# Buffers of keys, queries and values of branch A released by chunk, with the planner's constants set anew

## The chip, the cores and the metric

The kernel runs on one core of one Trainium2 chip. The metric is the device time of one execution in microseconds (us); less is better. A core has TensorE (PE in the profile; its weight loads are PEld), VectorE (DVE), ScalarE (ACT), GpSimd (POOL) and SyncE (SP, which here only issues DMAs). Each engine works through its own instructions in the order in which the program lists them and waits on semaphores for the others.

## The reference

Two attention branches are computed from two inputs of 2048 x 1024 in bf16, and their outputs are put side by side. Both have 32 heads of 32 channels.

```python
# branch A: plain attention, no mask
q, k, v = split(x @ wqkv)                    # 2048 x 1024 each
p = softmax(q @ k.T * 32 ** -0.5)            # 32 heads, 2048 x 2048
a = (p @ v) @ wo
# branch B: four segments of 512 rows, causal inside one, a memory M, z carried between them
p = softmax(qs @ ks.T * scale + mask)
a_mem = (phi(qs) @ M) / (phi(qs) @ z + 1e-6)
o = g * a_mem + (1 - g) * (p @ vs)
M, z = M + phi(ks).T @ vs, z + phi(ks).sum() # phi(t) = t + 1 if t > 0 else exp(t)
b = o @ wo
out = concat([a, b], -1)
```

## The kernel before

**What is computed where.** A head group is four heads, 128 channels; branch A has groups 0 to 7. A *unit* of branch A, written A(g, c), is 256 queries (chunk c of 8) of group g against all 2048 keys. It has eight *sets*; a set is 256 keys: four PE instructions write the scores of four heads to PSUM (line 960), two exps on ScalarE, of 128 x 1024 each, turn them into P (line 1039; line 1026 for the very first ones), and eight matmuls multiply P with the values (line 1135) and with ones (line 1142), which gives the row sums. In two or three sets of most units one of the four heads goes without ScalarE: a cubic on VectorE and GpSimd (lines 997, 1000 to 1002) stands for the exp, and ScalarE's instruction is half as long. A unit of branch B, B(s, j), is two head groups of one segment in five sets. Group 0's first four chunks are done in parts, since the input is still being loaded.

**Projections.** All other PE work is cut into *jobs* of eight steps with a 512-column moving operand: keys or queries of branch A (`job_KA(g, kq, c)`, four chunks c of 512 rows for keys, kq = 0, and four for queries, kq = 1), values (`job_VA`, `job_V0`), the same for branch B (`job_KB`, `job_VB`), and the two output projections (`job_outA`, `job_outB`). Jobs share one PSUM bank, so one job is open at a time; its result leaves by a DVE cast (line 1310), after which the bank is free.

**Buffers.** Keys and queries of group g lie in slot g % 2 of `KQ_A`, values of two groups in one of two `V_A`. So the projections of group g write where the keys and queries of group g - 2 stood. Each buffer has a record per chunk of 512 rows (`r_KQA[slot][kq][c]`), by which real dependencies are kept; but the planner offers all eight jobs of group g only from 2 us after the last unit of group g - 2, `r = en["A", g - 2, 7] + 2.0`, and a score set asserts with `holds` that all eight chunks carry the tag of its group.

**The guard.** Exps run without a shift as long as a bound on the scores says that this is safe. For each group the squares of keys and queries are made on GpSimd (line 1324, a ring of four tiles `sqA`), four of them are summed on PE and reduced on VectorE (`guard_cols`, lines 1335 and 1342), and when keys and queries are both there, `guard_end` (lines 1379 to 1413) spreads the maxima through PE and writes a flag. The first exp of the group waits until VectorE has written the flag (`run_split`): ScalarE loads it and branches. A late projection is therefore a late first exp of the group.

**The order of the work.** It is made when the program is built. `plan` sorts the units by a list of numbers: groups 0 to 5 in turn, then groups 6 and 7 interleaved as `PAIR` says, with the units of branch B put in at `B_FIRST`, `B_STEP`, `B_STEP3`, `B_GAP`. Each unit gets planned start and end times `st`, `en`. `plan_jobs` offers every job with a release time, a due time (`LEAD_A` = 14.219 us ahead of the group's first unit for keys and queries) and a cost of 1.75 us; `NUDGE` shifts due times by hand. `level` spreads the jobs so that the load is as even as the windows allow, and `Prog.schedule` then builds each engine's list with a model of durations and latencies; what PE takes next is ranked by `JOB_AT`, `JOB_SLOPE`, `DUE_AT`, `AHEAD`, `HEAT` and others. The weights of a group come by two DMAs on SP (`load_WA`), 10 us ahead of the release.

Near the end the units stand so: A(5,6), A(5,7), A(6,0), A(6,1), B(3,0), A(6,2), A(7,0), B(3,2), A(7,1), A(7,2), B(3,4), A(6,3), A(7,3), B(3,6), A(6,4), A(7,4), and so on to A(6,7), A(7,7). Between the end of group 5, which frees slot 1, and the first unit of group 7, which needs it, stand four units.

Of the kernel before, what the change touches and what calls it, by code (L numbers as in the profile page):

```python
# [33 lines left out]
CUBIC = [[], [1, 3], [2, 4], [1, 3], [1, 3], [1, 3], [1, 3], [1, 3], [1, 3], [1, 3], [1, 3], [1, 3], [1, 3], [1, 3], [1, 3], [1, 3, 5]]  # L34
CHAIN = 0
CUBE_PV = 3.203
# [3 lines left out]
SOON = 0.39  # L40

PAIR = ((6, 0), (6, 1), (6, 2), (7, 0), (7, 1), (7, 2), (6, 3), (7, 3), (6, 4), (7, 4), (6, 5), (7, 5), (6, 6), (7, 6), (6, 7),
        (7, 7))
# [6 lines left out]
B_STEP3 = 1.03  # L50
# [101 lines left out]
AHEAD = 18.672  # L152
HEAT = 0.757
# [5 lines left out]
NORM_K = 8.39  # L159
JOB_AT = 0.555  # L160
JOB_SLOPE = 0.737
MARGIN = 3.147
RXJ = 4
RX0 = 34.384
LEAD_A, LEAD_B, DUE_AT, DUE_SLOPE = 14.219, 8.77, 4.982, 0.1
# [4 lines left out]
STEP = 1.785  # L170
OUT3 = 87.197
OT_STEP = 2.92
NUDGE = {('KB', 3, 1): 8.43, ('VB', 1, 1): -8.13, ('OB', 0, 0): 8.85, ('OB', 2, 0): 12, ('KB', 1, 0): 7.83, ('OA', 4): -18.13, ('KB', 3, 0): -14.16, ('KA', 5): -2.7, ('KB', 3, 2): 0.67, ('OA', 3): -1.8, ('OA', 5): 0.15, ('VB', 0, 0): -25, ('phi', 3, 1): 6.17, ('KB', 3, 3): -2.7, ('KB', 2, 2): -3.03, ('OA', 0): 0.43, ('VB', 2, 0): 3.71, ('phi', 0, 1): -1.72, ('KB', 1, 1): -2.67, ('phi', 1, 1): 6.71, ('phi', 3, 3): 4.88, ('VB', 1, 0): -3.01, ('OB', 0, 1): 5.6, ('VB', 2, 1): 1.82, ('OB', 3, 0): 0.39, ('VB', 3, 1): -7.84, ('OB', 1, 1): 0.61, ('OB', 1, 0): 4.5, ('KB', 1, 2): -4.13, ('phi', 0, 0): 6.16, ('VB', 0, 1): 9.83, ('OB', 3, 1): -2.58, ('phi', 2, 2): -0.46, ('KB', 2, 1): 4.39, ('VA', 1): 6.19, ('KA', 2): -1.14, ('KA', 6): -6.01}
SAFE = 0
WOA_STEP = 3
OUT_D = 57.959
M_AT = 4.042

# [387 lines left out]
class _Kernel:  # L566
# [214 lines left out]
    def plan(self):  # L781
        self.plan_constants()
        T = 0.0
        self.st, self.en = {}, {}
        self.sets = {}
        self.slot_n = 0
# [129 lines left out]
    def plan_set(self, take, T):  # L916
# [16 lines left out]
        def f(key):  # L933
# [3 lines left out]
            for p in range(len(take[0]["pieces"])):  # L937
                for b, t in enumerate(take):
# [35 lines left out]
        u = take[0]["unit"]  # L974
        self.st.setdefault(u, T0)
# [541 lines left out]
    def job_KA(self, g, kq, c, key, behind=None):  # L1517
# [275 lines left out]
    def plan_jobs(self):  # L1793
# [13 lines left out]
        for c in (2, 3):  # L1807
            add(p2 - 3.9, p2 + 9.0, VJ, lambda key, c=c: self.job_V0(0, c, key, None, self.early_gc))
# [6 lines left out]
        for g in range(1, 8):  # L1815
            r = en["A", g - 2, 7] + 2.0 if g > 1 else 1.0
            d = st["A", g, 0] - LEAD_A
            for kq in range(2):
                self.item(r - 10.0 + kq * STEP, lambda key, g=g, kq=kq: self.load_WA(g, kq, key))
            for kq in range(2):  # L1820
                for c in range(4):
                    add(r, d, KQ, lambda key, g=g, kq=kq, c=c: self.job_KA(g, kq, c, key), "KA", g)
            add(r, d, 0.4, lambda key, g=g: self.guard_A(g, key + 2.0))
        for p in range(1, 4):
# [5 lines left out]
            for tp in range(8):  # L1830
                add(r, d, VJ, lambda key, p=p, tp=tp: self.job_VA(p, tp, key), "VA", p)
# [127 lines left out]
```

## Time and profile before

| | |
|---|---|
| median of 3 runs | 1118.94 us (1118.09 to 1119.88) |
| the profiled execution | 1119.28 us |
| its span, first to last instruction | 1117.6 us |
| ScalarE busy | 1068.5 us, 96% |
| TensorE busy | 1039.4 us, 93% |
| VectorE busy | 744.2 us, 67% |
| GpSimd busy | 675.6 us, 60% |
| mean granted TensorE clock | 0.996 |

The span is the time from the first to the last instruction of the profiled execution; 1.7 us of that execution lie around it. In a row of the timeline the columns are start, duration, engine, line, operation, output<-input, shapes, count, and in brackets the idle time of the engine before it with what ended it. A row of the waits has the waiting instruction, what it waited for, the total, the number of times and the longest. A row of the windows has the stretch, its length, and the busy time of each engine with its number of instructions, then the granted clock, the DMA share and the bandwidth. Rows of a line that is a helper (598 for the steps of all jobs, 1310 for all casts, 1324 for all squares) are told apart by the tiles.

### The profile page before, as it was taken

How to read it: one execution, taken by the hardware profiler on the slowest of the kernel's cores; microseconds unless marked ns; L12 is line 12 of the kernel's file. 1: busy time of each engine (PE TensorE's matmuls, PEld its weight loads, DVE VectorE, ACT ScalarE, POOL GpSimd, SP SyncE). 2: the span in 40 equal slices, each digit the busy share in tenths (PEclk: the TensorE clock that was granted, in tenths of full speed). 3: DMA queues.
4: the chain of work that ended last, by engine and by line, in shares of the span. 5: the costliest groups of instructions: out<-in, count | busy, mean ns of one | idle time of the engine just before them, and what ended most of it. 6: DMA issues, size and time to landing. Idle time of an engine off the chain costs nothing.

```text
span 1117.6 us, 55335 instructions
## 1 busy us (share of the span) xinstructions
PE 1039.4 (93%) x25336; PEld 555.5 (50%) x25336; DVE 744.2 (67%) x1567; ACT 1068.5 (96%) x1224; POOL 675.6 (60%) x654
## 2 busy tenths in 40 slices
PE   8999999999989989999999998989999889899997
PEld 4455545465545544455445444555555444444553
DVE  3346577765665686877875878697755777875443
ACT  4989999999999999999999999999999799999996
POOL 2224576856667576766666786676665857665530
PEclk9999999999999999999999999999999998999999
DMA  9032450024213231023241321033031450021101
GB/s 208 10 78 46 82 131 15 15 45 104 73 34 83 64 90 26 16 73 62 65 91 58 92 48 27 18 85 88 22 104 55 113 153 21 31 69 51 59 22 50
DMA packets 171099, 72.01 MB, mean 64 GB/s; under 512 B 134768, under 2 KB 169072, under 8 KB 170864
## 3 DMA queue, kind: packets, MB, share of 16 engines
q1 hardware_dynamic: 168496, 67.66, 24.6%
q8 instruction: 199, 3.26, 1.3%
q10 hardware_dynamic: 2368, 0.79, 0.3%
q14 instruction: 36, 0.29, 0.1%
HBM read 45.23 MB, written 11.67 MB: 51 GB/s over the span
## 4 chain that ended last, share of the span: by engine, by line
ACT 43%; PE 42%; DVE 11%; issue 2%; POOL 2%; ACTq 0%; DVEq 0%; POOLq 0%
ACT P L1039 41%; PE ps L598 22%; PE ps L960 8%; PE ps L1135 6%; PE ps L1142 5%; DVE Pc L1002 1%; DVE T L1160 1%; DVE PKQ_B L1605 1%; DVE rc L1167 1%; DVE Y L997 1%; ACT PKQ_B L1600 1%; PE ps L1556 1%; ACT P L1026 1%; DVE T L1163 1%; DVE outsb L1310 1%
## 5 line engine op out<-in xcount | busy, mean ns | idle before, releaser
L1039 ACT ACTIVATE P<-ps 128x1024 bf16<-128x1024 f32 (+1 forms) x1176 | 1041.2, 1078 | 27.4 <-PE ps L1142 11.3
L1142 PE MATMUL ps<-P,onesb 128*32 128x256 bf16 (+1 forms) x4628 | 298.0, 271 | 0.2 <-issue 0.2
L1000 POOL TENSOR_SCALAR Z<-Y 128x512 f32<-128x512 f32 x118 | 182.1, 1544 | 155.7 <-DVE Y L997 140.8
L1135 PE MATMUL ps<-P,V_A 128*32 128x256 bf16 x3860 | 255.0, 275 | 5.9 <-ACT P L1039 2.0
L960 PE MATMUL ps<-KQ_A 32*128 32x256 bf16 x4096 | 204.0, 273 | 24.2 <-ACT P L1039 17.6
L1001 POOL TENSOR_TENSOR Z<-Z,Y 128x512 f32<-128x512 f32 x118 | 152.0, 1288 | 4.1
L1142 PEld LDWEIGHTS ps<-P,onesb 128*32 128x32 bf16 x4628 | 129.6, 97 | 35.9 <-issue 13.5
L960 PEld LDWEIGHTS ps<-KQ_A 32*128 32x128 bf16 x4096 | 61.4, 92 | 167.9 <-ACT P L1039 129.5
L598 PE MATMUL ps<-xT_B,W_B 128*32 128x512 bf16 (+1 forms) x2240 | 138.1, 365 | 4.6 <-DVE cols L1396 1.3
L598 PE MATMUL ps<-xT_A,W_A 128*32 128x512 bf16 (+1 forms) x2224 | 136.9, 364 | 4.8 <-DVE KQ_A L1310 1.2
L1135 PEld LDWEIGHTS ps<-P,V_A 128*32 128x32 bf16 x3860 | 108.6, 96 | 45.6 <-issue 14.2
L1002 DVE SCALAR_TENSOR_TENSOR Pc<-Z,Y 128x512 bf16<-128x512 f32 x118 | 110.7, 938 | 26.3 <-POOL Z L1001 19.5
L997 DVE TENSOR_SCALAR Y<-ps 128x512 f32<-128x512 f32 x118 | 80.8, 685 | 67.3 <-PE ps L960 66.4
L1059 POOL TENSOR_SCALAR_AFFINE_SELECT P<-P 128x768 bf16<-128x768 bf16 (+1 forms) x96 | 78.0, 817 | 76.5 <-ACT P L1039 75.8
L1324 POOL TENSOR_TENSOR sqA<-KQ_A 128x512 bf16<-128x512 bf16 x61 | 66.0, 1084 | 91.3 <-DVE KQ_A L1310 68.4
L1324 POOL TENSOR_TENSOR sqB<-KQ_B 128x512 bf16<-128x512 bf16 x64 | 70.0, 1097 | 51.5 <-DVE KQ_B L1310 41.0
L1160 DVE STREAM_TRANSPOSE T<-ps 128x256 f32<-128x256 f32 (+1 forms) x148 | 71.5, 485 | 17.4 <-PE ps L1142 12.4
L598 PEld LDWEIGHTS ps<-xT_B,W_B 128*32 128x32 bf16 x2240 | 51.9, 96 | 55.1 <-issue 22.3
L598 PEld LDWEIGHTS ps<-xT_A,W_A 128*32 128x32 bf16 x2224 | 51.6, 96 | 54.5 <-issue 16.9
L1310 DVE CAST KQ_B<-ps 128x512 bf16<-128x512 f32 x64 | 44.0, 687 | 46.4 <-PE ps L598 45.0
L1175 DVE STREAM_TRANSPOSE T<-rc 128x256 f32<-128x256 f32 (+1 forms) x152 | 71.7, 477 | 2.4
L598 PE MATMUL ps<-Wv_B,xT_B 128*32 128x512 bf16 (+1 forms) x1120 | 68.5, 363 | 3.9 <-DVE V_B L1310 1.7
(106 smaller groups left out, 1316.9 us busy)
## 6 DMA issues: line engine op xcount, KB each, us to landing
Wv_B<-in_B_wv_dram SPq DMA_DIRECT2D x32, 256.0 KB, 3.0
W_B<-in_B_wk_dram SPq DMA_DIRECT2D x32, 256.0 KB, 3.2
W_B<-in_B_wq_dram SPq DMA_DIRECT2D x32, 256.0 KB, 4.1
Wo_B<-in_B_wo_dram SPq DMA_DIRECT2D x32, 256.0 KB, 3.0
out_dram<-outsb SPq DMA_DIRECT2D x56, 128.0 KB, 1.8
W_A<-in_A_wqkv_dram SPq DMA_DIRECT2D x14, 256.0 KB, 4.2
ot_a_scratch<-OTst SPq DMA_DIRECT2D x50, 64.0 KB, 2.3
xT_A<-ot_a_scratch SPq DMA_DIRECT2D x6, 512.0 KB, 4.4
```

Of the source, the lines that this page charges most:

```text
L598: ins = e.matmul(out[r], w[:, r], x, start=start, stop=stop, tile_position=(0, 32 * t), skip_group_check=True)
L960: ins = e.matmul(out, kap, qap, start=st, stop=True, tile_position=(32 * h, 0), skip_group_check=True)
L997: o = self.dve(lambda e: e.tensor_scalar(Y[:, :], src, KAPPA * SCALE, -KAPPA * ROOT, ALU.mult, ALU.add), 512, key - 9.0, [self.bank[bank]] ...
L1000: self.pool(lambda e: e.tensor_scalar(Z[:, :], Y[:, :], CUBE_A, None, ALU.add), 512, key - BCK, [rY], [rZ], rate=0.38)
L1001: self.pool(lambda e: e.tensor_tensor(Z[:, :], Z[:, :], Y[:, :], ALU.mult), 512, key - BCK, [rY, rZ], [rZ], rate=0.435)
L1002: last.append(self.dve(lambda e: e.scalar_tensor_tensor(out=dst, in0=Z[:, :], scalar=CUBE_B, in1=Y[:, :], op0=ALU.add, op1=ALU.mult), 512, ...
L1039: a = self.act(guarded if early else lambda e: e.activation(dst, src, ACT.Exp, scale=SCALE), cols, key, rd, wr, fixed=EXP_FIXED)
L1059: self.pool(lambda e: e.affine_select(v, v, pattern=pat, compare_op=ALU.is_ge, fill=0.0, base=0, channel_multiplier=-1), 2 * nd * P, key + ...
L1135: ins = e.matmul(self.ps[32 * h:32 * h + 32, 512 * obk + q0:512 * obk + q0 + nq], v, p, start=first, stop=last, tile_position=(0, 32 * h), ...
L1142: ins = e.matmul(self.ps[32 * h:32 * h + 32, lcol + q0:lcol + q0 + nq], self.onesb[:, 0:32], p, start=False, stop=last, tile_position=(0, ...
L1160: self.dve(lambda e: e.transpose(T2[:, 0:n], src), n, nk, rsrc, [r2], fixed=0.17)
L1324: self.pool(lambda e: e.tensor_tensor(sq[:, :], src, src, ALU.mult), 512, key, [rsrc], [rs], rate=0.5)
```

## The change

Keys, queries and values are offered to the next owner of their buffer by chunk. For g > 1 the release of a key chunk c (kq = 0) is the planned end of set 2c + 1 of the last unit of group g - 2, of a query chunk c (kq = 1) the planned end of unit A(g - 2, 2c + 1), each plus `FREED` = 0.5 us. The query chunks may so come up to one group sooner, the key chunks within the last unit of the old group. Value chunks are treated like key chunks with `VFREED`, and never later than before. The score sets assert only the chunks that they read. The four squares of a quad are put on record together when its fourth job is, so that the ring of four tiles is never shared by two quads at once; each square still needs only its own cast. The weights are loaded 10 us ahead of the first chunk of their own half. Apart from this, some fifteen constants of the planner and the table `NUDGE` have other values, among them `PAIR`, in which A(7,3) stands ahead of A(6,3), A(7,4) ahead of A(6,4) and A(7,5) ahead of A(6,5); by `B_STEP3`, B(3,6) stands one unit later. `CUBIC` is written in another way; its first two entries differ, but the first stands for the units in parts, which it does not reach, so that the number of half-length exps is the same (118 of 1184 exps).

```diff
-B_STEP3 = 1.03
+B_STEP3 = 1.073
...
-AHEAD = 18.672
-HEAT = 0.757
+AHEAD = 23.295
+HEAT = 0.681
...
-JOB_SLOPE = 0.737
+JOB_SLOPE = 0.617
...
-LEAD_A, LEAD_B, DUE_AT, DUE_SLOPE = 14.219, 8.77, 4.982, 0.1
+LEAD_A, LEAD_B, DUE_AT, DUE_SLOPE = 14.219, 8.77, 8.001, 0.1
...
-OUT3 = 87.197
+OUT3 = 72.703
...
+V0_R = 4.52
+V0_D = 11.868
+FREED = 0.5
+VFREED = 11.963
...
@@ plan_set
-                        holds([r for x in self.r_KQA[sl] for r in x], "KQ", g)
+                        holds([self.r_KQA[sl][0][kt // 4], self.r_KQA[sl][1][q // 512]], "KQ", g)
...
+        self.tset[take[0]["set"]] = T
@@ job_KA
-        q.append(self.square("A", dst, self.r_KQA[sl][kq][c], key + 1.5))
-        if len(q) == 4 and g > 0:
-            self.colA[(g, kq)] = self.guard_cols(key + 4.0, q)
+        q.append((dst, self.r_KQA[sl][kq][c], key + 1.5))
+        if g == 0:
+            q[-1] = self.square("A", *q[-1])
+        elif len(q) == 4:
+            self.colA[(g, kq)] = self.guard_cols(key + 4.0, [self.square("A", *x) for x in q])
@@ plan_jobs
         for c in (2, 3):
-            add(p2 - 3.9, p2 + 9.0, VJ, lambda key, c=c: self.job_V0(0, c, key, None, self.early_gc))
+            add(p2 - V0_R, p2 + V0_D, VJ, lambda key, c=c: self.job_V0(0, c, key, None, self.early_gc))
...
-            r = en["A", g - 2, 7] + 2.0 if g > 1 else 1.0
+            r = [[1.0] * 4] * 2
+            if g > 1:
+                r = [[self.tset["A", g - 2, 7, 2 * c + 1] + FREED for c in range(4)], [en["A", g - 2, 2 * c + 1] + FREED for c in range(4)]]
             d = st["A", g, 0] - LEAD_A
             for kq in range(2):
-                self.item(r - 10.0 + kq * STEP, lambda key, g=g, kq=kq: self.load_WA(g, kq, key))
-            for kq in range(2):
+                self.item((max(r[kq][0] - 10.0, q2) if g > 1 else r[kq][0] - 10.0 + STEP * kq), lambda key, g=g, kq=kq: self.load_WA(g, kq, key))
                 for c in range(4):
-                    add(r, d, KQ, lambda key, g=g, kq=kq, c=c: self.job_KA(g, kq, c, key), "KA", g)
+                    add(r[kq][c], d, KQ, lambda key, g=g, kq=kq, c=c: self.job_KA(g, kq, c, key), "KA", g)
+            r = max(r[0][3], r[1][3])
             add(r, d, 0.4, lambda key, g=g: self.guard_A(g, key + 2.0))
...
             for tp in range(8):
-                add(r, d, VJ, lambda key, p=p, tp=tp: self.job_VA(p, tp, key), "VA", p)
+                rt = self.tset["A", 2 * p - 3, 7, tp] + VFREED if p > 1 else r
+                add(min(r, rt), d, VJ, lambda key, p=p, tp=tp: self.job_VA(p, tp, key), "VA", p)
```

The other constants of the planner that change (`CUBE_PV`, `SOON`, `NORM_K`, `RX0`, `OT_STEP`, `OUT_D` and the `NUDGE` table) are left out here.

More of the change, by code (lines that the diff above doesn't have):

```diff
@@ L33 @@
 KAPPA, ROOT, CUBE_A, CUBE_B = 0.5501767600212002, -1.5993248390626598, -0.9857377158509045, 1.2295944671136563
-CUBIC = [[], [1, 3], [2, 4], [1, 3], [1, 3], [1, 3], [1, 3], [1, 3], [1, 3], [1, 3], [1, 3], [1, 3], [1, 3], [1, 3], [1, 3], [1, 3, 5]]
+CUBIC = ((1, 3), (1, 3), (2, 4), (1, 3), (1, 3), (1, 3), (1, 3), (1, 3), (1, 3), (1, 3), (1, 3), (1, 3), (1, 3), (1, 3), (1, 3), (1, 3, 5))
 CHAIN = 0
-CUBE_PV = 3.203
+CUBE_PV = 3.205
 CARRY = 7
@@ L39 @@
 BCK = 9.626
-SOON = 0.39
-PAIR = ((6, 0), (6, 1), (6, 2), (7, 0), (7, 1), (7, 2), (6, 3), (7, 3), (6, 4), (7, 4), (6, 5), (7, 5), (6, 6), (7, 6), (6, 7),
-        (7, 7))
+SOON = 0.124
+PAIR = ((6, 0), (6, 1), (6, 2), (7, 0), (7, 1), (7, 2), (7, 3), (6, 3), (7, 4), (6, 4), (7, 5), (6, 5), (6, 6), (7, 6), (6, 7), (7, 7))
 BIAS_PART = (17, 16, 18)
@@ L158 @@
 PV_HOT = 1.702
-NORM_K = 8.39
+NORM_K = 8.667
 JOB_AT = 0.555
-JOB_SLOPE = 0.737
+JOB_SLOPE = 0.617
 MARGIN = 3.147
 RXJ = 4
-RX0 = 34.384
-LEAD_A, LEAD_B, DUE_AT, DUE_SLOPE = 14.219, 8.77, 4.982, 0.1
+RX0 = 34.374
+LEAD_A, LEAD_B, DUE_AT, DUE_SLOPE = 14.219, 8.77, 8.001, 0.1
 HOLD = {}
@@ L785, in plan @@
         self.sets = {}
+        self.tset = {}
         self.slot_n = 0
```

6 lines of the change are left out of this document (3 added, 3 removed).

## The prediction

> **What bounds the kernel now.** I read the page first, then ScalarE's waits.
>
> ```profile
> PE 1039.4 (93%) x25336; PEld 555.5 (50%) x25336; DVE 744.2 (67%) x1567; ACT 1068.5 (96%) x1224; POOL 675.6 (60%) x654
> ACT  4989999999999999999999999999999799999996
> ```
>
> ScalarE is busy for 1068.5 of 1117.6 us, and its 40 slices show the idle time at the start, at the end, and in one slice of the middle, the seven. Nothing else can be gained as long as the exps stay what they are, and by the forms they are fixed in number and length:
>
> ```profile
> L1039 ACT ACTIVATE P<-ps 128x1024 bf16<-128x1024 f32 x1058 | 1006.2, 1123 | 26.1 <-PE ps L1142 11.3 <-PE ps L598 8.9 <-PE ps L960 3.2
> L1039 ACT ACTIVATE P<-ps 128x512 bf16<-128x512 f32 x118 | 80.3, 680 | 1.3 <-PE ps L960 1.3
> ```
>
> The change keeps 1058 full and 118 half exps and the 8 of line 1026. So the question is what becomes of ScalarE's waits:
>
> ```profile
> ACT P L1039 <- PE ps L1142: 11.3, 15, 2.9
> ACT P L1039 <- PE ps L598: 8.9, 1, 8.9
> ACT P L1039 <- PE ps L960: 4.5, 10, 1.1
> ```
>
> One single wait is 8.9 us; the other two rows, 15.8 us together, are 25 waits of at most 2.9 us. The timeline of ScalarE places the long one, and the timeline of all engines around it shows what came before. The 58 exps before it, counted back in the plan's order, are A(6,2), B(3,0), A(6,1) and A(6,0), so that the exp at 895.86 is the first of A(7,0), and group 5 ended at about 834.8.
>
> ```profile
> 884.85 0.68 DVE L1310 CAST KQ_A<-ps 128x512 bf16<-128x512 f32 x1
> ...
> 886.23 1.49 POOL L1324 TENSOR_TENSOR sqA<-KQ_A 128x512 bf16<-128x512 bf16 x1
> ...
> 887.14 1.90 PE L598 MATMUL ps<-xT_B,W_B 128*32 128x512 bf16 x32
> ...
> 889.09 0.69 DVE L1310 CAST KQ_B<-ps 128x512 bf16<-128x512 f32 x1 [2.07 <-PE ps L598]
> ...
> 889.84 0.40 PE L1335 MATMUL ps<-sqA,blk 128*32 128x512 bf16 x4 [0.47 <-DVE KQ_B L1310]
> ...
> 893.15 0.69 DVE L1310 CAST KQ_B<-ps 128x512 bf16<-128x512 f32 x1 [1.52 <-PE ps L598]
> ...
> 893.89 0.22 PE L1388 MATMUL ps<-pick,dg 128*32 128x16 bf16 x8 [0.79 <-DVE KQ_B L1310]
> ...
> 895.22 0.15 DVE L1413 SCALAR_TENSOR_TENSOR flags<-braw,flags 128x1 int32<-128x1 f32 x1
> ...
> 895.86 1.94 ACT L1039 ACTIVATE P<-ps 128x1024 bf16<-128x1024 f32 x2 [8.90 <-PE ps L598]
> ```
>
> This is the guard of group 7. Its eighth cast lands at 885.53 (884.85 + 0.68). Then follow the square, the sum on PE, which has to let a job of branch B through the only job bank first, another such job, the spread, and the flag at 895.37: 9.8 us from the cast to the flag. ScalarE was ready at 886.96 (895.86 - 8.90). The profile puts the wait down to a PE job, but it is the flag, 0.5 us ahead of the exp, that ended it.
>
> Why the cast is late is seen in the windows (stretch, PE, PEld, DVE, ACT, POOL):
>
> ```profile
> 728.00:756.00 28.00, 24.66 (x696) 14.84 (x688) 25.65 (x53) 27.49 (x32) 21.71 (x23) 1.00 0.35 90
> 756.00:784.00 28.00, 25.48 (x669) 14.43 (x668) 22.57 (x52) 27.74 (x33) 17.97 (x19) 1.00 0.34 83
> 784.00:812.00 28.00, 26.87 (x672) 14.10 (x668) 20.32 (x42) 27.88 (x34) 19.43 (x17) 1.00 0.12 28
> 812.00:834.80 22.80, 22.80 (x551) 12.16 (x547) 11.80 (x18) 22.76 (x27) 14.14 (x13) 1.00 0.44 118
> 834.80:868.00 33.20, 32.60 (x780) 17.16 (x776) 18.24 (x36) 33.13 (x38) 19.29 (x18) 1.00 0.18 55
> 868.00:887.00 19.00, 16.45 (x424) 8.68 (x424) 17.83 (x40) 18.95 (x23) 18.00 (x20) 1.00 0.51 129
> 887.00:895.90 8.90, 6.28 (x124) 3.14 (x124) 4.53 (x15) 0.04 (x1) 4.15 (x5) 1.00 0.15 51
> ```
>
> From 812 to 868 PE has 0.6 us of idle time in 56; ScalarE does not suffer there, but jobs queue. From 728 to 812 PE idles for 7.0 us (3.34 + 2.52 + 1.13), and none of group 7's work can go there, since all of it is held until group 5 is through. Inside the full stretch the eight casts stand so:
>
> ```profile
> 851.10 0.68 DVE L1310 CAST KQ_A<-ps 128x512 bf16<-128x512 f32 x1
> ...
> 861.07 0.69 DVE L1310 CAST KQ_A<-ps 128x512 bf16<-128x512 f32 x1 [1.12 <-PE ps L598]
> 867.49 0.69 DVE L1310 CAST KQ_A<-ps 128x512 bf16<-128x512 f32 x1 [0.89 <-PE ps L598]
> ```
>
> The first four begin at 851.10 and end with 861.07; the other four run from 867.49 to 884.85.
>
> **The change part by part.** *The query half of group 7 comes sooner.* A job is 32 matmuls; the one that starts at 887.14 takes 1.90 us, and since its end is modelled and overlaps what follows, I take 1.75 us of PE, an estimate. Four query jobs are 7.0 us of PE, four casts of 0.69, four squares. They may now start behind A(5,1), A(5,3), A(5,5) and A(5,7), which by the same count end at 729, 769, 807 and 835. The idle 7.0 us of 728 to 812 are what hides them, and group 6's own query jobs leave that stretch in turn for one earlier still. What is left after 834.8 is the key half: four jobs instead of eight. From the first cast to the eighth it is 33.8 us in seven steps, 4.8 us a step; four jobs less are worth 19 us at that pace, and 13.3 us at the pace of the first four (861.07 - 851.10 = 9.97 in three steps, 3.3 us each); I take the smaller. Either is more than 8.9. With the chain of 9.8 us behind the last cast, the flag would come at 895.37 - 13.3 = 882.1, ahead of ScalarE's 886.96 by 4.9 us. **The wait goes in full: -8.9 us.**
>
> *Is PE able to follow?* After 834.8 it has 7.0 us less to do, and the 2.6 us that it idled in the wait (8.90 - 6.28) need not be spent. That is 9.6 us, more than the 8.9 by which ScalarE is now ahead. So ScalarE can keep its lead to the end without a smaller idle share of PE.
>
> *What is late next.* The flag of B(3,2)'s guard.
>
> ```profile
> 898.79 0.15 DVE L1413 SCALAR_TENSOR_TENSOR flags<-braw,flags 128x1 int32<-128x1 f32 x1
> ```
>
> Its keys stand in the same queue, and the flag is 3.6 us behind that of group 7, at 898.9, while B(3,2), 16 exps behind the one at 895.86 and by the count at 909.5, would start at 900.6. That is 1.7 us to spare even if nothing ahead of it moves, and the four jobs that left move it forward too. I cost it at nothing; without that cover it is 3.3 us, one job step.
>
> *Weights, casts and squares.* The number is the same, the places move.
>
> ```profile
> L1324 POOL TENSOR_TENSOR sqA<-KQ_A 128x512 bf16<-128x512 bf16 x61 | 66.0, 1084 | 91.3 <-DVE KQ_A L1310 68.4
> W_A<-in_A_wqkv_dram SPq DMA_DIRECT2D x14, 256.0 KB, 4.2
> ```
>
> Twelve of the 14 weight loads on SP get another time, six of them a group earlier; one lands in 4.2 us and is asked for 10 us ahead, and the DMA share of 0.08 to 0.51 in the rows above leaves room, so nothing. On SP it passes output and scratch stores, which nobody waits for there. A square is 1.08 us on GpSimd, which had 91.3 us of idle time just before squares. A quad's ring tiles are handed out at its fourth job, so a fourth square can stand behind the previous quad's sum; with quads many microseconds apart I take 0, and at most the 1.49 us of one square in the chain above, which the 4.9 us cover.
>
> *Groups 2 to 6.* None of their guards shows a long wait, so sooner projections bring nothing there but fewer full stretches. The 15.8 us of small waits are made anew by another order. The early one and the one at the clock drop are singled out below; 11.4 us are left, and I take them as unchanged, with a quarter, 2.9 us, to both sides.
>
> *The start.* The retimed values job 2 of group 0 is on the path:
>
> ```profile
> 55.75 1.96 PE L1556 MATMUL ps<-Wv_A,xT_A 128*128 128x128 bf16 x32
> ...
> 58.49 0.29 PE L1135 MATMUL ps<-P,V_A 128*32 128x256 bf16 x4 [0.78 <-DVE V_A L1566]
> ```
> ```profile
> 59.16 3.77 ACT L1039 ACTIVATE P<-ps 128x1024 bf16<-128x1024 f32 x4 [2.88 <-PE ps L1142]
> 63.33 45.15 ACT L1039 ACTIVATE P<-ps 128x1024 bf16<-128x1024 f32 x51 [0.40 <-PE ps L1142]
> ```
>
> P waits for those values, and ScalarE for P's buffers: 3.3 us. The job is released 0.6 us sooner but is due 2.9 us later (11.868 against 9.0), while the rank of jobs changes too. Bounds: -3.3 (gone) and +2.9 (the later due time in full). I take 0, since the two edits pull apart.
>
> *The clock.* One stretch runs at half the clock:
>
> ```profile
> 924.00:928.00 4.00, 2.92 (x50) 1.04 (x46) 3.93 (x12) 4.00 (x6) 4.00 (x5) 0.62 0.60 131
> 928.00:932.00 4.00, 4.00 (x68) 2.05 (x68) 3.97 (x5) 3.18 (x4) 3.49 (x4) 0.53 0.00 0
> ```
> ```profile
> 932.26 29.08 ACT L1039 ACTIVATE P<-ps 128x1024 bf16<-128x1024 f32 x33 [0.95 <-PE ps L1142]
> ```
>
> It cost ScalarE 0.95 us there. In the new order it may fall away or come elsewhere: -1.0 to +1.0, taken as 0.
>
> *Sum.* 1119.28 - 8.9 = 1110.4 for an execution like the profiled one; that one lies 0.34 above the median of 1118.94, so **1110.0 us**, 0.8% less. With all small terms good it is 1110.0 - 3.3 - 1.0 - 2.9 = 1102.8, with all bad 1110.0 + 2.9 + 1.0 + 2.9 = 1116.8.
>
> **The rivals.** *Half of it comes* (0.14). The due time of group 7 is the same, 14.2 us ahead of its first exp, and the jobs that leave may be replaced: output and value jobs of branch B close up behind, and the planner spreads what is left up to the due time. If two of the four places are filled, the flag comes 6.7 us sooner instead of 13.3, the 8.9 become 2.2, and a later guard takes about the same again: 1110.0 + 4.4 = 1114.4. For it: the stretch from 812 to 868 is full. Against: nothing in the change brings branch B's jobs forward.
>
> *The clock drops in the full stretch* (0.05). By the half clock of 924 to 932, a stretch of 6.8 us at half speed puts PE 3.4 us behind; between 812 and 868, with 0.6 us of idle, all of it would reach ScalarE: 1113.4. [...] Against: the granted clock was 1.00 there, and 0.996 over the span. [...]
>
> *It doesn't do what it says* (0.06). The query jobs are offered sooner but the order built from ranks still takes them last, or the key half alone is late: 1119 us, within 0.2%.
>
> *Slower* (0.20). The release of a query chunk is 0.5 us behind the planned end of a unit, where before it was 2 us behind a whole group. Where PE runs behind the plan, the cast stands in VectorE's list before the scores that it waits for are done. Behind it in that list stands the cubic's first step (line 997), which frees a score bank, and behind that PE's next scores:
>
> ```profile
> 420.93 4.79 ACT L1039 ACTIVATE P<-ps 128x512 bf16<-128x512 f32 x6 [1.14 <-PE ps L960]
> ```
>
> This is ScalarE's price for one late score set at a half exp, 1.14 us. There are 24 query casts in groups 2 to 7 (six times four). If more than 8 hit (8 x 1.14 = 9.1), the gain is eaten; with half of them, 13.7 us, it is 1110.0 + 13.7 = 1123.7. For it: PE is 93% busy, with full stretches. Against: a release is no start; `level` puts most jobs well behind it, and VectorE is busy only 67%.
>
> **How the numbers follow.** The forecast has 0.55. Its own range is 1103 to 1117; the half, the clock and the rival without effect lie below 1121, and what is left out is the slower one: range 1103 to 1121. This kernel's measurement can tell about 0.2%, 2.2 us: faster, below 1116.7, is 0.55 + 0.14 + 0.05 = 0.74; same is 0.06; slower, above 1121.2, is 0.20.
>
> **What would show it.** Right: no wait of ScalarE over 3 us behind the start; the first exp of A(7,0) directly behind A(6,2), at about 887; its last KQ_A cast before 877 and its flag before 887; some KQ_A casts between 729 and 835 that belong to group 7; PE's idle time from 728 to 812 smaller, and that from 834.8 to 887 larger; 1058 and 118 exps. Wrong: a wait of several us at another group's first exp; ScalarE's many small waits clearly above 15.8 us, with VectorE casts of KQ_A that waited for line 960; a wait at 55 to 64 above 3.3 us.

## The result and the profile after

The changed kernel takes 1115.89 us (median of 16 runs, 1114.80 to 1118.98), the kernel before 1119.76 us (16 runs, 1117.77 to 1125.07). The ratio is 0.9963, with a 95% interval of 0.9954 to 0.9972: 3.9 us or 0.37% less. It is faster by more than the 0.2% that can be told, and the time lies inside the range of 1103 to 1121, but the gain is 0.37% where 0.8% was forecast.

The profiled execution took 1116.0 us, 3.3 us less than that of before. The page of the changed kernel (helpers have moved down a few lines: 598 is now 601, 960 is 964, 1039 is 1044, 1142 is 1147, 1310 is 1315, 1324 is 1329, 1335 is 1340, 1413 is 1418):

```profile
span 1114.3 us, 55312 instructions
PE 1035.5 (93%) x25332; PEld 558.1 (50%) x25332; DVE 732.8 (66%) x1567; ACT 1068.6 (96%) x1224; POOL 676.3 (61%) x654
ACT  4989999999999999999999999999999899999997
```

ScalarE does the same 1068.6 us of work. The slice that held the seven is an eight: the hole is smaller, not closed. ScalarE's waits on PE in its exps say why:

```profile
ACT P L1044 <- PE ps L1147: 19.5, 22, 3.7
ACT P L1044 <- PE ps L964: 4.8, 8, 1.7
```

The row of 8.9 us, one wait on a projection job, is gone. But the row for the ones matmul went from 11.3 to 19.5 us. A fourth row of the kernel before, at the start, has no counterpart now:

```profile
ACT P L1039 <- PE ps L1556: 1.4, 1, 1.4
```

Added up, these waits were 11.3 + 8.9 + 4.5 + 1.4 = 26.1 us and are 24.3 us. By this view little was gained. ScalarE's timeline shows where a part of it went:

```profile
883.38 2.15 ACT L1044 ACTIVATE P<-ps 128x1024 bf16<-128x1024 f32 x2
887.89 1.02 ACT L1044 ACTIVATE P<-ps 128x1024 bf16<-128x1024 f32 x1 [2.37 <-PE ps L1147]
890.61 7.01 ACT L1044 ACTIVATE P<-ps 128x1024 bf16<-128x1024 f32 x8 [1.70 <-PE ps L964]
```

The first exp of A(7,0) stands inside the last row, at 894.25, and waits for nothing. Just ahead of it, in A(6,2), ScalarE waits 2.37 + 1.70 = 4.07 us, where before it waited 0.02.

The exps are the same in number and, between the marks used here, in amount, so the starts of units can be compared across kernels. Counted off in the timeline (us; the last exp is its end):

| stretch | before | after | difference |
|---|---|---|---|
| start to A(0,4) | 79.63 | 80.34 | +0.71 |
| A(0,4) to A(6,0) | 755.17 | 758.41 | +3.24 |
| A(6,0) to A(7,0) | 61.06 | 55.50 | -5.56 |
| A(7,0) to the last exp | 211.91 | 212.21 | +0.30 |
| last exp to the end | 9.79 | 7.81 | -1.98 |
| sum | 1117.56 | 1114.27 | -3.29 |

The stretch that the change aims at gives 5.56 of the 8.9 us. The long stretch before it takes 3.24 back. Two of the 3.29 us come at the very end, where no exp is left.

**Group 7 in the new order.** VectorE's timeline, the casts of its keys and queries with what belongs to its flag:

```profile
827.13 0.68 DVE L1315 CAST KQ_A<-ps 128x512 bf16<-128x512 f32 x1
...
833.72 0.69 DVE L1315 CAST KQ_A<-ps 128x512 bf16<-128x512 f32 x1 [1.75 <-PE ps L601]
...
867.12 0.69 DVE L1315 CAST KQ_A<-ps 128x512 bf16<-128x512 f32 x1 [1.59 <-PE ps L601]
...
873.05 0.69 DVE L1315 CAST KQ_A<-ps 128x512 bf16<-128x512 f32 x1 [0.57 <-PE ps L601]
...
883.91 0.69 DVE L1315 CAST KQ_B<-ps 128x512 bf16<-128x512 f32 x1
...
885.19 0.69 DVE L1347 TENSOR_REDUCE cols<-ps 128x1 f32<-128x512 f32 x1 [0.30 <-PE ps L1340]
...
892.56 0.15 DVE L1418 SCALAR_TENSOR_TENSOR flags<-braw,flags 128x1 int32<-128x1 f32 x1
```

Three casts now begin between 827.13 and 833.72, ahead of A(6,0). Then come the four of the other quad, from 841.09 to 867.12, and last the one that was missing to the first quad. It ends at 873.74, 11.8 us sooner than the last cast of before (885.53). The flag lands at 892.71, just 2.7 us sooner than 895.37: from last cast to flag it is now 19.0 us, where it was 9.8. GpSimd's timeline shows most of what made the chain longer:

```profile
842.71 1.04 POOL L1329 TENSOR_TENSOR sqA<-KQ_A 128x512 bf16<-128x512 bf16 x1
...
876.69 3.05 POOL L1329 TENSOR_TENSOR sqA<-KQ_A 128x512 bf16<-128x512 bf16 x3
...
881.84 1.04 POOL L1329 TENSOR_TENSOR sqA<-KQ_A 128x512 bf16<-128x512 bf16 x1
```

The squares of the three early casts do not run at 828 to 835 but at 876.69, behind the sum of the other quad, which PE makes at 875.48: the ring's four tiles are handed out by quad, at the quad's fourth job, and this quad's fourth job is the last of the eight. The fourth square follows at 881.84, with other work of GpSimd between. From the last cast to the end of the last square it is 9.1 us, where it was 2.2 before (885.53 to 887.72): 7.0 of the roughly 9 us by which the chain grew. PE's timeline shows what follows:

```profile
884.75 0.40 PE L1340 MATMUL ps<-sqA,blk 128*32 128x512 bf16 x4 [0.89 <-POOL OT_B L1246]
885.94 1.04 PE L601 MATMUL ps<-xT_B,W_B 128*32 128x512 bf16 x8 [0.79 <-DVE cols L1347]
```

The sum comes 1.9 us behind its last square (882.88), because the job bank is held by a job of branch B until the cast of 883.91 ends at 884.60; the row names a store of GpSimd instead, which ended later, at 884.74, but reads and writes nothing of the sum. This step is no longer than before (2.1 us). Then PE stands still until VectorE has reduced the sum and the bank is free again. From the sum's start to the flag it takes 8.0 us instead of 5.5, the other 2.4 us. Behind the sum and the job in PE's list stand the matmuls with P, and ScalarE waits for those: the 2.37 us. Part of it is the clock (stretch, PE, PEld, DVE, ACT, POOL, clock):

```profile
884.00:888.00 4.00, 2.46 (x32) 1.21 (x36) 3.69 (x7) 1.63 (x3) 4.00 (x5) 0.73 0.49 135
888.00:892.00 4.00, 4.00 (x104) 2.26 (x100) 3.41 (x7) 2.30 (x3) 4.00 (x5) 0.84 0.22 50
```

The missing clock is 4 x (0.27 + 0.16) = 1.7 us, that is 3.4 us at half speed: the granted clock is 0.50 from 885.86 to 889.28 us.

### The profile page after: what moved, and what is told of

It reads as the page before. It is cut to its first block, busy times and chain, and to the rows that moved or that the text cites. A ratio compares the mean times of both kernels' runs of the same rounds, so it can differ in the third digit from the quotient of the medians.

```text
span 1114.3 us, 55312 instructions
## 1 busy us (share of the span) xinstructions
PE 1035.5 (93%) x25332; PEld 558.1 (50%) x25332; DVE 732.8 (66%) x1567; ACT 1068.6 (96%) x1224; POOL 676.3 (61%) x654
## 4 chain that ended last, share of the span: by engine, by line
ACT 44%; PE 40%; DVE 8%; POOL 4%; issue 2%; SPq 1%; DMA 0%; ACTq 0%; DVEq 0%
ACT P L1044 42%; PE ps L601 19%; PE ps L964 8%; PE ps L1140 6%; PE ps L1147 5%; PE ps L1563 1%; POOL Z L1005 1%; DVE Pc L1007 1%; ACT PKQ_B L1607 1%; DVE PKQ_B L1612 1%; SPq L1284 1%; DVE rc L1172 1%; POOL Z L1006 1%; DVE Y L1002 1%; POOL P L1064 1%
## 5 line engine op out<-in xcount | busy, mean ns | idle before, releaser
L1044 ACT ACTIVATE P<-ps 128x1024 bf16<-128x1024 f32 (+1 forms) x1176 | 1041.9, 1084 | 25.7 <-PE ps L1147 19.5
L1147 PEld LDWEIGHTS ps<-P,onesb 128*32 128x32 bf16 x4628 | 129.4, 97 | 36.2 <-issue 13.3
L1007 DVE SCALAR_TENSOR_TENSOR Pc<-Z,Y 128x512 bf16<-128x512 f32 x118 | 105.2, 892 | 21.4 <-POOL Z L1006 14.8
L1165 DVE STREAM_TRANSPOSE T<-ps 128x256 f32<-128x256 f32 (+1 forms) x148 | 71.9, 487 | 21.3 <-PE ps L1147 12.9
L601 PEld LDWEIGHTS ps<-xT_A,W_A 128*32 128x32 bf16 x2236 | 52.0, 96 | 53.2 <-issue 15.8
```

The costliest lines, as they stand in the source:

```text
L601: ins = e.matmul(out[r], w[:, r], x, start=start, stop=stop, tile_position=(0, 32 * t), skip_group_check=True)
L1007: last.append(self.dve(lambda e: e.scalar_tensor_tensor(out=dst, in0=Z[:, :], scalar=CUBE_B, in1=Y[:, :], op0=ALU.add, op1=ALU.mult), 512, ...
L1044: a = self.act(guarded if early else lambda e: e.activation(dst, src, ACT.Exp, scale=SCALE), cols, key, rd, wr, fixed=EXP_FIXED)
L1147: ins = e.matmul(self.ps[32 * h:32 * h + 32, lcol + q0:lcol + q0 + nq], self.onesb[:, 0:32], p, start=False, stop=last, tile_position=(0, ...
```

## The experiments

Two theories stood against each other for the middle. **The chain**: the release does its work, but the guard is still held up, because the ring of squares is given out by quad. **The order**: the wait is not worth what it looks like, since every re-laid order makes new waits elsewhere. A third question was the end. All ratios are to the kernel before on the same chip, with 95% intervals.

### What the guard's wait is worth

Both kernels, with this edit:

```diff
@@ guard_A
-        self.guard_end(key + 0.2, [self.colA[(g, 0)], self.colA[(g, 1)]], 1, [g % 2])
+        if g < 7:
+            self.guard_end(key + 0.2, [self.colA[(g, 0)], self.colA[(g, 1)]], 1, [g % 2])
@@ job_KA
+        if g == 7:
+            return
```

The return stands ahead of the squares, so the guard's work on GpSimd, PE and VectorE goes together with its wait.

> The kernel before without the guard of group 7: its eight squares, two sums and the flag are left out, and the exps of group 7 go by the flag of the groups before. Theory: the wait of 8.9 us at the first exp of A(7,0) was worth what the prediction took it for, and PE can follow: 8 to 10 us less, ratio 0.991 to 0.993. Rival: another limit stands just behind it (PE's full stretch, the guards of branch B): 3 to 6 us less, ratio 0.9945 to 0.997.

Measured 1114.73 us (4 runs, 1110.78 to 1118.15), ratio 0.9952 (0.9935 to 0.9969). The four runs scatter; the profiled one is the fastest, so its trace tells more of the place than of the size. ScalarE's timeline there:

```profile
878.70 21.86 ACT L1039 ACTIVATE P<-ps 128x512 bf16<-128x512 f32 x25
```

It runs through the spot without a stop. A(7,0) begins at 887.32, 8.5 us sooner; A(6,0) to A(7,0) takes 51.71 us against 61.06, and the last exp ends 7.8 us sooner. So in this execution the 8.9 us were real, and PE could follow when they went, as forecast. The ratio lies in the rival's range (0.9945 to 0.997) all the same: the theory holds in the trace of the fastest run and not in the times of the four. A part of that is behind the last instruction: 3.0 to 3.1 us of each of these runs lie around the span, against 1.7 in the kernel before, as the last section tells.

> The changed kernel with the same part left out, the guard of group 7. Theory: the two new waits of ScalarE in A(6,2), 2.4 and 1.7 us, come from that guard (its squares late on GpSimd, its sums in PE's list ahead of P times values, and the clock that halves in the gap), so that 2.5 to 4.5 us go against the changed kernel, ratio to the kernel before 0.992 to 0.994; and it stays slower than the kernel before without its guard, by the some 4 us that the changed kernel loses before group 6. Rival: these waits come from the crowd of VectorE and GpSimd work in that stretch, guard or not: within 1 us of the changed kernel, ratio 0.995 to 0.997.

Measured 1117.92 us (10 runs, 1116.55 to 1121.00), ratio 0.9972 (0.9961 to 0.9983): no better than the changed kernel itself (0.9963), and the expectation fails. In the trace the spot does improve, and that part of the theory holds: the wait in A(6,2) falls from 4.07 to 0.84 us, and A(6,0) to A(7,0) from 55.50 to 53.20. But behind A(7,0) it takes 214.59 us instead of 212.21. What is won in the middle is given back later. The next run shows one place.

### The queries of group 7 kept together

```diff
-                    add(r[kq][c], d, KQ, lambda key, g=g, kq=kq, c=c: self.job_KA(g, kq, c, key), "KA", g)
+                    add(r[kq][c], d - 0.5 * (kq == 1 and g == 7), KQ, lambda key, g=g, kq=kq, c=c: self.job_KA(g, kq, c, key), "KA", g)
```

> The changed kernel with the due time of group 7's query jobs 0.5 us ahead of that of its key jobs, nothing else. In the changed kernel three query chunks of group 7 were cast at 827 to 834, the fourth only at 873, behind all four key chunks. As the four squares of a quad get their ring tiles at its fourth job, the three early squares waited until the other quad was summed (875.5), and ran at 876.7 to 879.7; from the last cast to the flag it took 19.0 us instead of 9.8 before. Theory: this split of the quad is what stretched the chain and put the guard's sums in PE's way; with all queries first the squares of three chunks no longer wait for the other quad, last cast to flag takes 8 to 12 us, and ScalarE's waits in A(6,2), 4.1 us, fall below 1.5. What becomes of the whole time is open by the theory, since everything behind is laid anew: ratio 0.993 to 0.999. Rival: the chain is long because GpSimd and VectorE are full in that stretch: cast to flag still 15 us or more and A(6,2) still waits over 3 us.

Measured 1117.73 us (10 runs, 1115.93 to 1121.55), ratio 0.9966 (0.9950 to 0.9983). VectorE's timeline:

```profile
863.55 0.69 DVE L1347 TENSOR_REDUCE cols<-ps 128x1 f32<-128x512 f32 x1 [0.73 <-PE ps L1340]
...
874.49 0.69 DVE L1315 CAST KQ_A<-ps 128x512 bf16<-128x512 f32 x1 [1.43 <-PE ps L601]
...
886.71 0.99 DVE L1418 SCALAR_TENSOR_TENSOR flags<-braw,flags 128x1 int32<-128x1 f32 x1
```

The first four casts (827.63 to 841.58) are now one quad, summed at 863. The last cast comes 1.4 us later than in the changed kernel, and the flag 5.0 us sooner: 12.5 us from cast to flag instead of 19.0, a little above the 8 to 12 expected. ScalarE's timeline:

```profile
884.57 3.77 ACT L1044 ACTIVATE P<-ps 128x1024 bf16<-128x1024 f32 x4 [0.89 <-PE ps L1147]
...
892.12 8.42 ACT L1044 ACTIVATE P<-ps 128x1024 bf16<-128x1024 f32 x10 [0.51 <-PE ps L1147]
...
1051.12 56.30 ACT L1044 ACTIVATE P<-ps 128x1024 bf16<-128x1024 f32 x64 [1.41 <-PE ps L1147]
```

The chain theory holds at its spot: 0.89 us of waiting in A(6,2), and 52.88 us from A(6,0) to A(7,0). And the time does not fall: 215.30 us follow behind A(7,0), with waits of 3.93 us there against 0.87. The largest, 1.41 us at 1051, also shows in the changed kernel without group 7's guard, at 1050.55. It lies where PE is nearly full. The windows of this run say so:

```profile
1020.00:1050.00 30.00, 29.38 (x688) 14.84 (x688) 13.52 (x24) 29.57 (x34) 13.65 (x12) 1.00 0.24 73
1050.00:1080.00 30.00, 29.61 (x724) 15.93 (x716) 13.59 (x23) 28.88 (x34) 10.09 (x8) 1.00 0.09 30
```

PE is busy for 58.99 of 60 us at the full clock, and for 7.85 of the 8 us around the wait (1044 to 1052); in the changed kernel it is busy for 60.00 of these 60 us. That a ScalarE which comes there sooner has to wait is likely, but argued: the kernel before without group 7's guard comes there sooner still and does not wait at that place, and its order is another one. This wait is 1.41 of the 3.93 us; four others of 0.16 to 0.96 us, each for PE, make up most of the rest.

### Release and constants apart

The first kernel has the release by chunk with every old constant (only values of later groups come 0.5 us behind the old group's end, where before it was 2 us), the second the new constants with the old release (`r = [[en["A", g - 2, 7] + 2.0] * 4] * 2`, values, squares and weights as before). The third is the kernel before with the keys and queries of group 7 due 2 us sooner (`NUDGE` of `('KA', 7)` lowered by 2.0).

> The release by chunk alone: all constants, PAIR, B_STEP3, NUDGE and the windows of the values of group 0 as before (for the values of later groups the old release). Theory: the release takes the 8.9 us wait away or shortens it, but it lays all jobs of groups 2 to 7 anew, and the old constants fit the old order; the waits that come up elsewhere cost more than it gains: 3 to 15 us slower than before, ratio 1.003 to 1.013. Rival: the release alone carries the gain and the constants are trimming: ratio 0.993 to 0.998.

Measured 1134.17 us, ratio 1.0116 (1.0102 to 1.0131). ScalarE's waits in its trace:

```profile
ACT P L1045 <- PE ps L1148: 34.5, 27, 6.7
```

The 8.9 us at A(7,0) are 0.80, but A(6,2) waits 8.25 us and the stretch from A(0,4) to A(6,0) 26.23 instead of 12.33. The release alone is a loss of 1.2%.

> The changed kernel's constants, PAIR and B_STEP3 with the old release (2 us behind the whole of group g - 2, for keys, queries and values), the old load times and the squares put on record one by one. Theory: the constants fit the new release alone; the wait for the guard of group 7 comes back (6 to 12 us at the first exp of A(7,0)) and the time is 3 to 13 us above before, ratio 1.003 to 1.012. Rival: the new constants carry the gain and the release is not needed: ratio 0.994 to 0.999.

Measured 1128.88 us, ratio 1.0061 (1.0043 to 1.0079). Its waits:

```profile
ACT P L1044 <- PE ps L601: 6.1, 1, 6.1
```

The wait of A(7,0) is back with 6.1 us, A(6,2) waits 3.00, and the long stretch 17.75; another 4.8 us stand ahead of a short ScalarE instruction of branch B, at 902.56. So neither half is the gain; only together do they beat the kernel before.

> The kernel before with one due time changed: that of group 7's keys and queries 2 us sooner. Theory: what was lost against the forecast (waits of about 1 us each, made anew in places that the release does not concern) is the price of any new order, since the order before was fitted by many constants; so even this edit, which should help the late guard of group 7, costs 3 to 10 us, ratio 1.003 to 1.009, in many waits of ScalarE of about 1 us. Rival: an order is robust against such edits, and a due time 2 us sooner takes up to 2 us off the 8.9: ratio 0.998 to 1.0.

Measured 1131.08 us, ratio 1.0086 (1.0068 to 1.0104). With one due time moved, the long stretch waits 23.95 us, A(5,4) alone 5.92, so not only in waits of about 1 us, and A(7,0) still 4.14. This is for the order theory: one number that seems local lays the jobs of many groups anew, and these three kernels come out 7 to 13 us slower as long as the other constants stay.

### Both kernels with constants fitted once more

A random search over the planner's constants moved 17 of them and 21 entries of `NUDGE` in the changed kernel (`LEAD_A` 14.93, `LEAD_B` 9.01, `B_GAP` 3.337 and others), and 14 constants and 18 entries in the kernel before. Among the 17 is one of the release itself: `FREED` went from 0.5 to -0.285, so that chunks are offered 0.8 us sooner. How far each search went is not on record.

> The changed kernel, its structure untouched, with the planner's constants and due times fitted once more (a random search over the same constants that the change moved and some of their neighbours, by the planner's own model of the order). Theory: what the change lost against the forecast is the order, not the release: the small waits of about 1 us and the two waits in A(6,2) can be had smaller with the release as it is. Then ScalarE's waits between 80 us and the last exp fall from the 20.6 of the changed kernel to under 14, and the time is 5 to 11 us below before, ratio 0.990 to 0.9955. Rival: these waits follow from the release (casts, squares and jobs crowding in front of the scores) and stay: ratio 0.995 to 0.998.

Measured 1111.06 us (5 runs, 1107.47 to 1111.65), ratio 0.9888 (0.9869 to 0.9907): faster than both kernels. ScalarE's waits:

```profile
ACT P L1044 <- PE ps L1147: 13.1, 12, 3.6
...
ACT P L1044 <- PE ps L964: 2.5, 6, 0.9
```

From A(0,4) to A(6,0) it waits 9.79 us, less than the kernel before (12.33), in A(6,2), which here stands ahead of B(3,0), not at all, in A(7,0) 0.86. Between 80 us and the last exp that makes 12.9 us, under the 14 of the theory; the ratio is a little better than its range. A(6,0) to A(7,0) takes 50.74 us, 10.3 less than before; 3.5 us more than before are lost at the start and 3.3 more behind A(7,0). The guard's chain is no shorter here: three squares again stand behind the other quad's sum, and from the last cast (ends 847.84) to the flag (872.18) it takes 24.3 us. But the last cast comes 37.7 us sooner than in the kernel before, so the flag is there 13.4 us ahead of A(7,0).

> The kernel before with the old release and the same fitting of its constants. Theory: without the release the guard of group 7 can be moved only at the cost of other jobs; a wait of 3 us or more stays at the first exp of A(7,0), and the kernel comes out above the refitted changed kernel by 2 to 6 us, ratio to before 0.994 to 0.999. Rival: the release is not needed, constants alone take the wait away: the two refitted kernels are within 1.5 us of each other.

Measured 1116.01 us (5 runs, 1115.14 to 1116.73), ratio 0.9944 (0.9931 to 0.9958). Its waits:

```profile
ACT P L1039 <- PE ps L1142: 13.4, 15, 2.2
...
ACT P L1039 <- PE ps L598: 4.0, 1, 4.0
```

With the old release this fit shortens the wait at A(7,0) to 4.0 us and does not take it away. A part of its gain is the end: the traced span is 3.4 us shorter than in the kernel before on the same chip, and 2.0 of them lie behind the last exp (7.83 instead of 9.85), while 0.9 us more lie around the span. With both sides fitted the release by chunk is worth 1116.01 - 1111.06 = 5.0 us, and the intervals do not touch; the ends differ by 0.3 us only. This is one fit of each; a longer search could move either.

### The end, and how far one trace is to be trusted

> The kernel before once more, for its profile. [...]

Measured 1119.22 us. The five stretches of the table above come out as 79.58, 755.41, 61.09, 211.56 and 9.85: within 0.35 us each of the first execution. ScalarE's two closing waits stand 2.14 us apart (1114.89 and 1117.03), with a packet of the instruction queue between them at 1115.51; in the first execution it was 2.06 us (1115.03 and 1117.09).

> The changed kernel once more, for its profile. Theory: the closing waits again 0.07 us apart and 7.8 us from the last exp to the end; the wait in A(6,2) again about 4 us with half a clock window beside it; the start of A(6,0) about 4 us later than in the kernel before on the same chip. Rival: these are accidents of one execution and differ by more than 1 us.

Measured 1118.8 us, 2.8 more than the profiled one. The end is 7.81 us again. The start is 0.6 longer and A(0,4) to A(6,0) 3.1 longer (761.49), with the clock at half for 3.4 us near 171 and again near 413, where the first execution had none; A(6,2) waits 2.89, at the full clock. A(6,0) begins 7.5 us later than in the second execution of the kernel before, where 4 were expected; so two of the four things expected came out off by over 1 us, as the rival has it. The long stretch waits 17.98 us here and 15.61 in the first execution. The same jobs there in the two experiments on the changed kernel gave 15.42 without a drop of the clock and 15.77 with one, at 410. The kernel before gave 12.33, 12.50, without the guard 12.40, and 13.58 in the run that follows. So the changed order waits longer there in every trace, by 1.8 to 5.7 us.

The last one puts 16 waits that are long satisfied into ScalarE's list near its start, so that all that follows stands further on (in the trace they are eight instructions, 1381 of ScalarE against 1373; two waits that follow each other directly start 0.09 us apart in the trace of the kernel before, eight times):

```diff
+                        count += 1
+                        if count == 4:
+                            for _ in range(16):
+                                eng.wait_ge(self.sems["POOL"], 1)
```

> The kernel before with 16 waits more in ScalarE's list, all on a semaphore that has long been up, placed in its idle time at the start (each some 0.05 us); nothing else changes. Theory: the last 2.0 us that the change gained are not in the work. [...] Then the span ends 1.5 to 2.1 us earlier than before, ratio 0.998 to 0.9987, with the closing waits under 0.2 us apart. Rival: the closing 2 us are the landing of the last outputs, or an accident of one execution; then 0 to +1 us, ratio 1.000 to 1.001.

Measured 1121.29 us against 1121.34 for the kernel before, ratio 0.9995 (0.9981 to 1.0010). In the trace the end falls from 9.79 to 7.80 us and the closing waits stand 0.07 us apart (1118.61 and 1118.68) instead of 2.06, as in the changed kernel (7.81 and 0.07): the 2.0 us hang on where ScalarE's closing instructions lie, not on the change's subject. The time does not show it. The same trace is 1.5 us longer up to A(0,4) and 1.4 longer to A(6,0), and whether that is the shift's own price or this execution's isn't settled. What the end is worth in the median stays open.

## Why the prediction was right and wrong

**"The wait goes in full: -8.9 us."** The row is gone, and the kernel before without the guard's work shows its worth in the trace of its fastest run: 8.5 us at A(7,0), 7.8 at the last exp. What failed is the step to it: "with the chain of 9.8 us behind the last cast". The cast came 11.8 us sooner, near the 13.3 that I took, but the chain became 19.0. I had seen the cause and priced it wrong: "a fourth square can stand behind the previous quad's sum; I take 0, and at most the 1.49 us of one square". Four squares stood there, since the planner split the quad of the first three casts, and the lead of 4.9 us that was to cover it was spent. The queries kept together show it: 12.5 us, and the flag 5.0 us sooner. The refitted kernel shows the other way out: its chain is 24.3 us long, and costs nothing, since its last cast comes 37.7 us sooner and not 13.3.

**What stood in its place** was not a wait at the flag but 4.07 us in A(6,2), on PE's list: sum and jobs stand there ahead of the matmuls with P, and GpSimd (4.00 of 4 us) and VectorE (3.69 of 4) were full. From 8.9 to 4.07 is 4.8 us; the stretch won 5.56, since one of its two short ScalarE instructions for branch B (0.7 to 0.8 us) now stands elsewhere.

**"None of their guards shows a long wait, so sooner projections bring nothing there", and 11.4 us of small waits "taken as unchanged", within 2.9.** They grew by 3.28 us from A(0,4) to A(6,0) (12.33 to 15.61), a little beyond the bound. This is the second term that was mis-sized. (The waits that the prediction sets aside, 3.3 and 0.95 us, leave 11.6 of the 15.8 and not 11.4; that changes nothing.) I priced an order by its list of edits; in three experiments an order laid anew came out 7 to 13 us slower with constants that were not fitted to it, and 3.3 is what was left after the fit that came with the change. In the refitted kernel it is below zero (9.79). Which edit makes which of these small waits is not shown.

**"The idle 7.0 us of 728 to 812 are what hides them."** They do not. The windows of the changed kernel, same columns as before:

```profile
728.00:756.00 28.00, 25.57 (x752) 16.71 (x744) 23.48 (x58) 26.96 (x32) 20.09 (x22) 1.00 0.40 83
756.00:784.00 28.00, 26.32 (x728) 15.84 (x724) 19.18 (x45) 27.82 (x32) 15.68 (x17) 1.00 0.39 93
784.00:812.00 28.00, 24.82 (x616) 12.60 (x616) 18.09 (x44) 26.41 (x32) 19.17 (x18) 1.00 0.06 19
812.00:834.80 22.80, 22.80 (x544) 11.91 (x544) 12.60 (x23) 22.77 (x27) 12.36 (x10) 1.00 0.38 96
834.80:868.00 33.20, 33.14 (x812) 17.95 (x808) 16.39 (x31) 33.13 (x39) 16.42 (x15) 1.00 0.13 41
868.00:887.00 19.00, 15.21 (x328) 6.56 (x324) 16.82 (x39) 17.52 (x21) 16.69 (x18) 0.97 0.48 120
```

PE idles for 2.43 + 1.68 + 3.18 = 7.3 us from 728 to 812, where I had written "smaller". The three queries came at 827, 24 us sooner and not a group sooner, inside the stretch that was full already: it still has 0.06 us of idle time in 56. A release is no start, as I wrote of the rival; I did not apply it to my own term.

**"PE is able to follow"** is right for the kernel before without its guard (212.67 us behind A(7,0), 0.8 more than with it). In the changed order it holds less: the three kernels that clear the middle, the refitted one among them, lose 2.4 to 3.1 us behind A(7,0) against the changed kernel, in part where PE is busy for some 59 of 60 us.

**The start**, taken as 0 between -3.3 and +2.9, gave +0.7. (The DMA share in the rows that the prediction shows up to there is 0.12 to 0.51, not 0.08; nothing hangs on it.) **The clock**, taken as 0 within 1.0: the drop left 924 to 932 (0.50 for 6.8 us) and came at 886 to 889 (0.50 for 3.4 us), where ScalarE waited already. Its share of the 4.07 us is about 1.2, an estimate: in the second execution, at the full clock there, A(6,2) waits 2.89.

**The end** was not in the sum, and gave -1.98 of the profiled -3.29 us. So the exps' own path won 1.3 us in this pair of executions. The forecast's direction is right; whether it would be by over 0.2% without the end is open. That the time lies inside the forecast's own 1103 to 1117 is luck in part: these bounds were drawn for the small terms around a gain of 8.9 us, and it was the large term that came out smaller.

**The rivals.** "Half of it comes" gave 1114.4 and is near in time, and it is right that branch B's jobs close up: of their key and query jobs 116 matmuls, some 3.6 jobs, now run between 834.8 and 887, where before there was none. But only one of these jobs has its cast ahead of group 7's last one (at 837.10), so that still came 11.8 us sooner. What ate it was the flag's chain, with two of these jobs ahead of its sum: the flag came 2.7 us sooner instead of 6.7 or 13.3. So the time that this rival names is near by luck. "It doesn't do what it says" holds for the idle stretch, not for the casts. The clock did not drop in the full stretch: it was 1.00 from 812 to 868 in the changed kernel as in the kernel before. The slower rival's late casts do not show: the casts of keys and queries in VectorE's list waited for PE's jobs, one of them for a matmul with P (0.8 us), and none for scores; the eight of group 7 waited at most 1.75 us; and the ACT row for scores went from 4.5 to 4.8 us. Slower kernels there were, at 1.0061 to 1.0116, by a mechanism that I had not listed: waits spread over groups 1 to 6.

**The signs.** No wait over 3 us behind the start: right, at most 2.37. A(7,0) directly behind A(6,2): right, but at 894.25 and not 887. Last cast before 877: right. Flag before 887: wrong. Casts of group 7 ahead of 835: right for three. Idle time of PE from 834.8 to 887: 3.85 us against 3.15, hardly larger.

## What to carry to other kernels

Where an order is laid by a planner, price a new release by the wait that it takes away and, apart from that, by an order laid anew: try it with constants fitted for both sides, or the comparison measures the fit. When a buffer is given back in smaller pieces, look at what follows it in the chain (here the ring of squares, the job bank, the sum) and whether that is still given out in the old pieces. And follow a freed wait to the end of the kernel: what ScalarE wins in the middle (55.50 to 53.20 us in the changed kernel without group 7's guard) it can lose in later stretches (212.21 to 214.59 us there) where PE has hardly a pause.

## What the hardware showed that was not expected

**The last instructions take 2 us more in one of the orders.** ScalarE's closing instructions, starts in us; the last output had landed at 1114.70 (before) and 1113.38 (after):

```
                        before   before, again   after   after, again   before, shifted
jump to closing code    1112.16     1112.03     1110.86     1113.67        1115.75
first closing wait      1115.03     1114.89     1113.73     1116.53        1118.61
second closing wait     1117.09     1117.03     1113.80     1116.61        1118.68
```

From the jump to the next instruction it is 2.9 us in all five, and 2.8 to 3.0 in all 13 traces of this case; in each of them a packet of 8192 B of queue 14, which the profile calls an instruction queue, starts 1.3 us behind the jump. Between the two waits it is 2.1 us in the kernel before and 0.1 in every other one, and only in the kernel before a second such packet stands between them, at 1115.64 (1115.51 in the second execution). The profile does not say for which engine a packet is; that this one loads ScalarE's instructions and that ScalarE waits for it is read from its place and not shown. What the traces show is that from the last exp to the end it is 9.79 and 9.85 us with the second packet and 7.81, 7.81 and 7.80 without it, and that with eight instructions more in the list neither the packet nor the 2.1 us is there. Something similar shows behind the span, though no run was made for it: the kernel before without the guard and both refitted ones have two packets of that queue behind their last instruction, the others one, and in each of their runs 2.1 to 3.1 us lie around the span, where it is 1.7 to 1.9 in all others.

**The clock drops move.** In two executions of one kernel the clock was halved at other places: 886 to 889 in the one, near 171 and 413 in the other. The one at 886 lasts 3.41 us, the one at 924 in the kernel before 6.83 us, twice as long, both at 0.50. PE was not idle throughout ahead of the one at 886: in the 3.41 us up to 885.86 it was busy for 1.79 us. Ahead of the 16 drops in this case's traces it was 1.2 to 2.1 us of 3.41, so each follows a thin stretch; but a stretch as thin (1.78 us from 887.6 in the second execution) passed without one, and what brings a drop is not shown. The row at 924 that the prediction reads lies mostly inside its drop; in the 3.41 us ahead of it, up to 924.96, PE was busy for 2.08 us.
